# Column-norm attention with a soft mixture of experts on one core: two softmax steps and two small scalings change engine, a fold and a product change form, and the order changes

## The chip, the cores and the metric

The kernel runs on one core of one Trainium2 chip. The core has a matrix engine (TensorE, PE in the profile), a vector engine (VectorE, DVE), an activation engine (ScalarE, ACT), a general engine (GpSimd, POOL), a queue engine that here issues every DMA (SyncE, SP), 24 MB of on-chip memory with 128 partitions (SBUF), and eight accumulator banks (PSUM). The metric is the device time of one execution in microseconds (us); lower is better.

## What is computed

```python
def _attn_ref(q, k, v, tau):            # B, N, C = 4, 5056, 256
    qn = q / (np.linalg.norm(q, axis=1, keepdims=True) + 1e-06)
    kn = k / (np.linalg.norm(k, axis=1, keepdims=True) + 1e-06)
    s = kn.transpose(0, 2, 1) @ qn / tau        # 256 x 256 for each batch
    a = softmax of s over its last axis
    return v @ a                                # x of the next function

def _moe_ref(x, phi, w1, w2):           # x: 20224 rows, 8 experts of 4 slots
    logits = x @ phi                            # 20224 x 32
    d = softmax of logits over the rows
    slot_input = d.T @ x                        # 32 x 256
    h = np.maximum(slot_input[e] @ w1[e], 0.0)  # each expert e, 256 -> 1024
    slot_out[e] = h @ w2[e]                     # 1024 -> 256
    c = softmax of logits over the 32 slots
    return c @ slot_out                         # 20224 x 256
```

All of it is float32. The softmax over the rows needs every row before the experts can begin, and the output needs the experts.

## The kernel before

The rows of q and k come in 40 units of 512 rows, ten for each of the four batches, each as one tile `raw` of 1 MB (two of 0.75 MB). The rows of v come in 20 pairs of 1024 rows, five for each batch (`v`, 1 MB, and for ten of them also a transposed copy `x` read from memory; the other ten are turned by TensorE into tiles `T` and copied to `x` by DVE and ACT). Then come 8 MB of expert weights (`w1`, `w2`) in, and 20.7 MB of output out.

**For each unit** ACT casts `raw` to a rounded high part `hl` (L278), POOL subtracts to get the low part (`low`, L282, 128 partitions x 512 elements a time), ACT squares (L293), DVE adds the squares into two PSUM accumulators `A` (L311), and PE multiplies k by q into the 256 x 256 scores `S` (L335). Some tiles skip the split and go in as plain float32.

**For each batch** the norms are taken, DVE scales the scores (`ssb`, L397) and takes the row maxima (`nm`, L400), ACT takes the exponential (`a`, L406), PE transposes it (`aTp`, L423) and multiplies it with phi (`Mp`, L435), so that the logits of a pair are one product of `x` and `M` (L502), without v @ a ever being formed.

**For each pair** the logits `L` go through ACT and DVE: copies, running maxima, a 32 x 32 stream transpose into `nat` (`logit_nat`, L535; one tile of 128 x 1280 for each batch, 40 groups of 32 slots), exponentials and weights `dn`; PE gathers dn.T @ v (`gather`, L602). At a batch's end the gathered 128 x 256 sum `gs` is folded from four groups of partitions to one (`finish_fold`, L623: two matmuls with a matrix `fold` of four stacked identities), scaled on DVE (`gts`, L629), multiplied with `a` (`sp`, L643) and added to `acc` (L649, L651). For the last batch `acc` is scaled by `be` (L637) and `rz` is formed from the denominators (L668 to L670).

**The softmax over slots**, for each batch on its whole `nat`, has six steps: `c_max` (DVE, L691), `c_sub` (DVE, L694: `nat` minus its maxima broadcast over 32 slots), `c_exp` (ACT, L697), `c_sum` (DVE, L701), `c_rec` (ACT and DVE, L705, L706), `c_mul` (DVE, L709), and then five transposes `c_flip` into `cT` (L721). The maxima `cm` and the sums `cs` have one buffer each for all four batches.

**The tail**: `slT` (L684, L685) holds the transposed slot inputs; `up` is the first expert product (`H`, L746, 64 matmuls), `relu` on ACT (`hs`, L758), `flip_h` and `back_h` (`hTp`, `hT`, L764, L770), `down` in two channel halves (`O0`, `O1`, L779), a copy `ob` (L791), a fold (L795) and `so` (L801), and then the output product of `cT` and `so` (`out_mul`, L817), with evictions by DVE and ACT (L834) and stores (L838 to L843). Batch 0 is stored by channel halves, so that the first half of its output can leave when `O0` is done and before `O1`: tiles `oh` of two pairs and one half, 1 MB (the fifth pair 0.5 MB a half). The other batches are stored as whole pairs `o` of 1 MB.

**What sets the order.** Nothing is scheduled by a rule: the work is a plan of 1201 steps, and a list `ORDER` of their numbers, written out, is the order in which each engine gets its instructions. `SLOTS` gives each large tile one of 23 slots of 8 KB a partition, `BANKS` each PSUM tile one of eight banks. A tile waits for the last users of its slot or bank. All DMAs are issued from SP in `ORDER`'s sequence; each also waits for the DMA eight before it (eight semaphores in turn, DMAHW0 to 7), so a waiting load holds up all behind it. The host lays the inputs out and puts the output's rows back in place.

Of the kernel before, what the change touches and what calls it, by code (L numbers as in the profile page):

```python
# [11 lines left out]
ALU = mybir.AluOpType  # L12
# [155 lines left out]
def colnorm_attention_soft_moe(  # L168
# [450 lines left out]
    def finish_fold(b):  # L619
        gs = st[b]["gs"]  # L620
        gt = bank(f"gt{b}")[:, : 2 * S].rearrange("p (m s) -> p m s", m=2)
        for m in range(2):
            pe.matmul(gt[:, m, :], gs[:, P * m : P * m + P], fold, start=True, stop=True)  # L623
        st[b]["gt"] = gt
# [439 lines left out]
```

## Time and profile before

| | |
|---|---|
| time, median of 3 runs | 280.41 us (280.21 to 280.92) |
| the profiled execution | 280.04 us, of which the span of its trace is 278.1 us |
| busy: PE, DVE, ACT, POOL | 245.0, 219.8, 205.0, 152.6 us |
| DMA | 110.81 MB, mean 398 GB/s over the span |
| read, written | 89.43 MB, 20.97 MB |

The span is the part of the execution that the trace covers; 1.94 us of the profiled execution lie outside it. The engines' busy times overlap, so that they don't add up to the span, and an engine that is busy is not therefore what the end waits for. In the stretches the DMA share is that of sixteen DMA engines that is busy, and the granted clock of TensorE is in shares of full speed (1.00 is 2.4 GHz, 0.50 is 1.2 GHz).

### The profile page before, as it was taken

Reading aid. Unit: us, or ns where it says so; the run is one execution under the profiler, and the core shown is the slowest. Engines: PE = TensorE matmul, PEld = TensorE weight load, DVE = VectorE, ACT = ScalarE, POOL = GpSimd, SP = SyncE. Lnnn points to the kernel's source line nnn. Section 1 sums busy time; section 2 is a strip of 40 time slices with the busy share of each in tenths; the row PEclk is TensorE's granted clock in tenths of the full one; section 3 lists DMA queues with packets and bytes.
Section 4 is the critical chain, followed back from the end, with each engine's and each line's share of the span. In section 5 each row is a group of like instructions: output and inputs, shape, how many; then the busy total and the mean of one; then the engine's idle time right before and its main releaser. Section 6 shows DMA issues by size and latency. Waiting matters only on the chain.

```text
span 278.1 us, 6508 instructions
## 1 busy us (share of the span) xinstructions
PE 245.0 (88%) x2568; PEld 207.8 (75%) x2568; DVE 219.8 (79%) x405; ACT 205.0 (74%) x321; POOL 152.6 (55%) x127
## 2 busy tenths in 40 slices
PE   7999999999999999999992999999999899997000
PEld 6899988999989969798791979996645787765000
DVE  1397498988898998999999999998789969866300
ACT  4999899999999999989963959773727326663200
POOL 1699899999889989999991677600000000000000
PEclk9999999999999999999998699999999999999755
DMA  7999999999999999999999989999999379999996
GB/s 279 430 424 420 420 420 417 421 417 422 420 421 420 422 420 422 413 419 421 417 421 420 415 333 407 428 422 415 416 424 417 132 308 372 411 414 418 424 418 263
DMA packets 15727, 110.81 MB, mean 398 GB/s; under 512 B 1873, under 2 KB 1873, under 8 KB 3025
## 3 DMA queue, kind: packets, MB, share of 16 engines
q1 hardware_dynamic: 15696, 110.40, 96.1%
q8 instruction: 20, 0.33, 0.5%
q14 instruction: 11, 0.08, 0.1%
HBM read 89.43 MB, written 20.97 MB: 397 GB/s over the span
## 4 chain that ended last, share of the span: by engine, by line
PE 40%; DMA 15%; DVE 11%; ACT 11%; POOL 9%; issue 7%; DVEq 0%; ACTq 0%; POOLq 0%
PE S L335 17%; DMA raw<-in_qk_dram 10%; POOL hl L282 9%; PE op_None L817 6%; DVE A L311 5%; DMA w<-in_moe_w_dram 4%; ACT hl L278 4%; PE T L482 4%; ACT sq L293 4%; PE L L502 3%; PE G L602 3%; PE O L779 3%; PE op L817 2%; DVE o L834 2%; ACT o L834 1%
## 5 line engine op out<-in xcount | busy, mean ns | idle before, releaser
L282 POOL TENSOR_TENSOR hl<-raw,hl 128x512 fp32r<-128x512 f32 x117 | 148.2, 1312 | 25.0 <-ACT hl L278 24.4
L311 DVE TENSOR_TENSOR A<-sq,A 128x512 f32<-128x512 f32 (+1 forms) x144 | 94.1, 690 | 20.0 <-ACT sq L293 18.0
L335 PE MATMUL S<-hl 128*128 128x256 f32 x702 | 101.7, 295 | 0.2 <-POOL hl L282 0.2
L335 PEld LDWEIGHTS S<-hl 128*128 128x128 f32 x702 | 90.5, 193 | 3.6 <-issue 2.0
L293 ACT ACTIVATE sq<-raw 128x2048 f32<-128x2048 f32 (+2 forms) x40 | 71.9, 1812 | 0.0
L278 ACT CAST hl<-raw 128x1024 fp32r<-128x1024 f32 (+1 forms) x69 | 61.1, 925 | 2.8 <-DMA raw<-in_qk_dram 1.5
L335 PE MATMUL S<-raw 128*128 128x256 f32 x156 | 38.3, 381 | 0.8 <-DMA raw<-in_qk_dram 0.8
L335 PEld LDWEIGHTS S<-raw 128*128 128x128 f32 x156 | 27.7, 190 | 4.2 <-DMA raw<-in_qk_dram 1.1
L834 DVE COPY o<-op_None 128x512 f32<-128x512 f32 x30 | 18.9, 683 | 7.3 <-PE op_None L817 6.5
L834 ACT COPY o<-op_None 128x512 f32<-128x512 f32 x30 | 15.9, 594 | 10.8 <-PE op_None L817 9.8
L482 PE MATMUL T<-ident,v 128*128 128x128 f32 x156 | 22.9, 281 | 0.0
L602 PE MATMUL G<-v,dn 128*32 128x256 f32 x312 | 19.8, 381 | 0.0
L502 PE MATMUL L<-x,M 128*32 128x256 f32 (+1 forms) x320 | 19.0, 378 | 0.1
L482 PEld LDWEIGHTS T<-ident,v 128*128 128x128 f32 x156 | 18.6, 144 | 0.4
L817 PE MATMUL op_None<-so,cT 32*128 32x256 f32 x160 | 17.8, 405 | 0.4
L817 PEld LDWEIGHTS op_None<-so,cT 32*128 32x128 f32 x160 | 12.1, 183 | 4.8 <-DVE o L834 1.9
L602 PEld LDWEIGHTS G<-v,dn 128*32 128x32 f32 x312 | 11.8, 109 | 4.9
L502 PEld LDWEIGHTS L<-x,M 128*32 128x32 f32 x320 | 9.8, 110 | 6.5 <-issue 0.3
L694 DVE TENSOR_TENSOR nat<-nat,cm 128x1280 f32<-128x1280 f32 x4 | 14.4, 3603 | 0.1
L487 DVE COPY x<-T 128x512 f32<-128x512 f32 x20 | 13.1, 680 | 0.6 <-PE T L482 0.6
L487 ACT COPY x<-T 128x512 f32<-128x512 f32 x20 | 11.3, 588 | 2.3 <-PE T L482 2.3
L817 PE MATMUL op_None<-so,nat 32*128 32x256 f32 x80 | 9.2, 404 | 2.0 <-ACT o L834 0.9
(119 smaller groups left out, 265.2 us busy)
## 6 DMA issues: line engine op xcount, KB each, us to landing
raw<-in_qk_dram SPq DMA_DIRECT2D x38, 1024.0 KB, 13.5
v<-in_v_dram SPq DMA_DIRECT2D x16, 1024.0 KB, 11.6
w<-in_moe_w_dram SPq DMA_DIRECT2D x16, 1024.0 KB, 11.8
out_dram<-o SPq DMA_DIRECT2D x15, 1024.0 KB, 9.6
x<-in_vt_dram SPq DMA_DIRECT2D x10, 1024.0 KB, 13.5
out_dram<-oh SPq DMA_DIRECT2D x4, 1024.0 KB, 5.1
v<-in_v_dram SPq DMA_DIRECT2D x4, 896.0 KB, 15.1
raw<-in_qk_dram SPq DMA_DIRECT2D x2, 768.0 KB, 14.1
```

What stands on the lines that cost most here:

```text
L278: act.copy(parts(u, lo, hi)[:, :, 0::2, :], raws[u][:, lo:hi])
L282: pool.tensor_tensor(hl[:, :, 1::2, :], raws[u][:, lo:hi], hl[:, :, 0::2, :].bitcast(F32), op=ALU.subtract)
L293: act.activation(sqs[u][:, n : NT[u]], raws[u][:, n : NT[u]], AF.Square)
L311: dve.tensor_tensor(a[r], s[r, j], a[r], op=ALU.add)
L335: pe.matmul(S_[:, m], l, r, start=first, stop=False, skip_group_check=True)
L482: pe.transpose(tp[:, P * jj : P * jj + P], vtile(p, 4 * h + jj)[:, P * m : P * m + P], ident)
L487: to(xt(p)[:, m, h * UT : h * UT + UT], tps[p, h, m])
L502: pe.matmul(L[S * g : S * g + S, :n, :], M[:, m, :], x[:, :n, S * g : S * g + S], start=m == 0 and g not in void, stop=m == 1, skip_group_ ...
L602: pe.matmul(gp[S * g : S * g + S, :C], dn[:, x, j, :], vtile(p, j), start=x == 0 and j < G, stop=x == n - 1 and j >= G,)
L694: dve.tensor_tensor(nat[b], nat[b], st[b]["cm"].broadcast_to([P, 8 * PB, S]), op=ALU.subtract)
L817: pe.matmul(ops[b, p, hf, g][:, h, :], cT[b][r, 4 * i : 4 * i + 4, :].rearrange("s j t -> s (j t)"), rhs[r], start=True, stop=True,)
L834: (dve.tensor_copy if g % 2 else act.copy)(dst, ops[b, p, hf, g])
```

## The change

`ORDER`, `SLOTS` and `BANKS` are replaced as a whole. Beside that:

- `c_sub` and `c_mul` go from DVE to POOL, in all four batches.
- The scaling of `acc` by `be` in the last batch and that of `sel_sb` to `rz` go from DVE to ACT.
- `finish_fold` for batches 0 to 2: PE transposes the two halves of `gs` into the bank, and DVE sums the four groups there (a reduction to 128 x 64 from 128 x 256); batch 3 keeps the two matmuls with `fold`.
- `out_mul` for the channel halves: the weights are now the half of `so` (32 x 128) and the moving side is 256 columns of `cT`, so that the result has channels on the partitions; 4 matmuls of 256 columns for a pair and half in place of 8 of 128. Tiles, evictions and stores keep their sizes; the host puts the result in place by another transpose.

```diff
 ORDER = [
-    2, 0, 1, 23, 6, 7, 8, 49, 3, 5, 4, 9, 24, 32, 25, 28, 26, 27, 10, 50, 33, 34, 51, 55, 56, 58, 54, 57, 52,
...
+    2, 3, 0, 1, 6, 8, 4, 7, 9, 5, 23, 32, 24, 25, 26, 33, 29, 49, 28, 30, 50, 51, 56, 54, 55, 10, 11, 12, 18,
...
     def finish_fold(b):
         gs = st[b]["gs"]
-        gt = bank(f"gt{b}")[:, : 2 * S].rearrange("p (m s) -> p m s", m=2)
+        tr = bank(f"gt{b}")
+        st[b]["gt"] = gt = tr[:, C : C + 2 * S].rearrange("p (m s) -> p m s", m=2)
         for m in range(2):
-            pe.matmul(gt[:, m, :], gs[:, P * m : P * m + P], fold, start=True, stop=True)
-        st[b]["gt"] = gt
+            if b < B - 1:
+                pe.transpose(tr[:, P * m : P * m + P], gs[:, P * m : P * m + P], ident)
+            else:
+                pe.matmul(gt[:, m, :], gs[:, P * m : P * m + P], fold, start=True, stop=True)
+        st[b]["tr"] = tr[:, :C].rearrange("p (m g s) -> p m s g", m=2, g=G)
 
     def finish_mul(b):
         gts = bpool.tile([P, 2, S], F32, tag="gts", name=f"gts{b}")
+        if b < B - 1:
+            dve.tensor_reduce(st[b]["gt"], st[b]["tr"], axis=AX.X, op=ALU.add)
         for m in range(2):
...
         if b == B - 1:
-            dve.tensor_scalar_mul(acc, acc, be[:HD])
+            act.mul(acc, acc, be[:HD])
...
-        dve.tensor_scalar_mul(rz, sel_sb, zs)
+        act.mul(rz, sel_sb, zs)
...
     def c_sub(b):
-        dve.tensor_tensor(nat[b], nat[b], st[b]["cm"].broadcast_to([P, 8 * PB, S]), op=ALU.subtract)
+        pool.tensor_tensor(nat[b], nat[b], st[b]["cm"].broadcast_to([P, 8 * PB, S]), op=ALU.subtract)
...
     def c_mul(b):
-        dve.tensor_tensor(nat[b], nat[b], st[b]["cs"].broadcast_to([P, 8 * PB, S]), op=ALU.mult)
+        pool.tensor_tensor(nat[b], nat[b], st[b]["cs"].broadcast_to([P, 8 * PB, S]), op=ALU.mult)
...
     def out_mul(b, p, hf):
-        n = C if hf is None else P
+        so = now["so"]
+        if hf is not None:
+
+            for g in range(G):
+                r = slice(S * g, S * g + S)
+                ops[b, p, hf, g] = bank(f"op{b}_{p}_{hf}_{g}")[:, : 8 * S]
+                pe.matmul(
+                    ops[b, p, hf, g],
+                    so[r, hf],
+                    cT[b][r, 8 * p : 8 * p + 8, :].rearrange("s j t -> s (j t)"),
+                    start=True,
+                    stop=True,
+                )
+            return
         for g in range(G):
-            ops[b, p, hf, g] = bank(f"op{b}_{p}_{hf}_{g}")[:, : 2 * n].rearrange("p (h c) -> p h c", h=2)
-        so = now["so"]
-        rhs = so.rearrange("s x c -> s (x c)") if hf is None else so[:, hf]
+            ops[b, p, hf, g] = bank(f"op{b}_{p}_{hf}_{g}").rearrange("p (h c) -> p h c", h=2)
+        rhs = so.rearrange("s x c -> s (x c)")
```

What the new order moves is shown at three places. In these rows `hl_...`, `raw_...`, `nat_...` are tiles with the program's own numbers, and a line number is that of the kernel whose row it is. `nat_82` and `nat_83` are `nat` of batches 0 and 1; in the kernel after, `nat_2118` and `nat_2432` are those of batches 2 and 3.

**VectorE at the slot softmax of batch 1**, in the kernel before, around the scaling of batch 2's scores (`ssb`, `nm`):

```order
L584 STREAM_TRANSPOSE dn_1_1776<-lt_1_1737 128x512
L311 TENSOR_TENSOR A_0_1475<-sq_1727,A_0_1475 128x512
L649 COPY acc<-sp_1758 64x256
L694 TENSOR_TENSOR nat_83<-nat_83,cm_1671 128x1280
L311 TENSOR_TENSOR A_1_1477<-sq_1699,A_1_1477 128x512
L397 SCALAR_TENSOR_TENSOR ssb_1591<-ssb_1591,rk_1806,rq_1808 128x256
L400 TENSOR_REDUCE nm_1811<-ssb_1591 128x1
```

And VectorE in the kernel after, at the same scaling of batch 2's scores:

```order
L396 SCALAR_TENSOR_TENSOR ssb_1818<-ssb_1818,rk_1869,rq_1862 128x256
L399 TENSOR_REDUCE nm_1871<-ssb_1818 128x1
L654 COPY acc<-sp_1820 64x256
L310 TENSOR_TENSOR A_1_1370<-sq_1910,A_1_1370 128x512
L616 SCALAR_TENSOR_TENSOR gs_1884<-gs_1884,al_1964,G_1_1940 128x256
L696 TENSOR_REDUCE cm_1985<-nat_83 128x40
L310 TENSOR_TENSOR A_0_1368<-sq_1758,A_0_1368 128x512
L310 TENSOR_TENSOR A_1_1370<-sq_1981,A_1_1370 128x512
L310 TENSOR_TENSOR A_0_1368<-sq_1805,A_0_1368 128x512
L416 RECIPROCAL sm_1933<-sm_1933 128x2
```

The subtraction of `nat_83` no longer stands ahead of the scaling, nor on VectorE at all; the maxima of batch 1 (`cm_1985`) now stand behind the scaling, and since `cm` has one buffer they wait for GpSimd's subtraction of batch 0.

**GpSimd from the place where `c_sub` of batch 0 now stands**, in the kernel before the last rows of its program:

```order
L282 TENSOR_TENSOR hl_1960<-raw_1629,hl_1960 128x2x256
L282 TENSOR_TENSOR hl_1962<-raw_1668,hl_1962 128x2x256
L282 TENSOR_TENSOR hl_2071<-raw_1464,hl_2071 128x2x256
L282 TENSOR_TENSOR hl_2077<-raw_1668,hl_2077 128x2x256
L282 TENSOR_TENSOR hl_2071<-raw_1464,hl_2071 128x2x256
L282 TENSOR_TENSOR hl_2174<-raw_1694,hl_2174 128x2x256
L282 TENSOR_TENSOR hl_2177<-raw_1694,hl_2177 128x2x256 x2
L282 TENSOR_TENSOR hl_2174<-raw_1694,hl_2174 128x2x256
L373 TENSOR_TENSOR rn_2200<-rn_2200,half 128x4
```

And GpSimd in the kernel after:

```order
L281 TENSOR_TENSOR hl_1853<-raw_1620,hl_1853 128x2x256
L699 TENSOR_TENSOR nat_82<-nat_82,cm_1366 128x1280
L281 TENSOR_TENSOR hl_1969<-raw_1569,hl_1969 128x2x256
L281 TENSOR_TENSOR hl_1966<-raw_1638,hl_1966 128x2x256 x2
L281 TENSOR_TENSOR hl_2013<-raw_1630,hl_2013 128x2x256
L281 TENSOR_TENSOR hl_1969<-raw_1569,hl_1969 128x2x256
L281 TENSOR_TENSOR hl_2013<-raw_1630,hl_2013 128x2x256
L281 TENSOR_TENSOR hl_2065<-raw_1569,hl_2065 128x2x256 x2
L281 TENSOR_TENSOR hl_1853<-raw_1620,hl_1853 128x2x256
L281 TENSOR_TENSOR hl_2104<-raw_1620,hl_2104 128x2x256
L372 TENSOR_TENSOR rn_2135<-rn_2135,half 128x4
L281 TENSOR_TENSOR hl_2104<-raw_1620,hl_2104 128x2x256
```

The subtraction of batch 0's maxima now stands among the last subtractions of the units, with twelve of them behind it (the twelfth, `hl_2122<-raw_1638`, follows the last row above) and the root of batch 3 (`rn`). Behind that stand the other seven, in this order: `c_sub` of batch 1, `c_mul` of 0, `c_mul` of 1, `c_sub` of 2, `c_sub` of 3, `c_mul` of 2, `c_mul` of 3. On ScalarE the exponential of batch 2's `nat` now stands between `rz` and the four `relu`, and that of batch 3 behind them; both wait for GpSimd.

**SyncE where the last v and the weights are loaded**, with what each load waits for, in the kernel before:

```order
L458 DMA v_2377<-in_v_dram 128x2048 [waits DMAHW1_49,PE_49,Activation_49]
L738 DMA w_0_0_2470<-in_moe_w_dram 128x2048 [waits DMAHW2_49,DVE_49,Activation_49]
L733 DMA w_2_2635<-in_moe_w_dram 128x2048 [waits PE_49,DMAHW3_49,Activation_49,Pool_49]
L733 DMA w_0_2637<-in_moe_w_dram 128x2048 [waits DMAHW4_49,PE_49,Pool_49]
L733 DMA w_4_2657<-in_moe_w_dram 128x2048 [waits DMAHW5_49,PE_49]
```

And in the kernel after:

```order
L457 DMA v_2458<-in_v_dram 128x2048 [waits DMAHW1_49,PE_49]
L743 DMA w_0_3_2587<-in_moe_w_dram 128x2048 [waits DMAHW2_49,Pool_49]
L738 DMA w_3_2638<-in_moe_w_dram 128x2048 [waits DMAHW3_49,PE_49]
L738 DMA w_1_2640<-in_moe_w_dram 128x2048 [waits DMAHW4_49,PE_49]
L738 DMA w_2_2642<-in_moe_w_dram 128x2048 [waits DMAHW5_49,PE_49]
L738 DMA w_4_2670<-in_moe_w_dram 128x2048 [waits DMAHW6_49,PE_49]
```

The load behind the last v now takes the slot that the last subtraction on GpSimd (`hl_2122`) used and waits for it, and six loads of `w1` stand behind it on the queue. In both kernels the last `raw` is the 58th or 59th DMA, the last v the 74th and the last `w1` the 81st, then seven `w2`, then the stores.

## Rows read from the trace of the kernel before

**Rows 1.** The page: busy time of each engine, and what the DMAs moved in each of 40 equal slices of the span.

```profile
PE 245.0 (88%) x2568; PEld 207.8 (75%) x2568; DVE 219.8 (79%) x405; ACT 205.0 (74%) x321; POOL 152.6 (55%) x127
...
GB/s 279 430 424 420 420 420 417 421 417 422 420 421 420 422 420 422 413 419 421 417 421 420 415 333 407 428 422 415 416 424 417 132 308 372 411 414 418 424 418 263
```

**Rows 2.** Stretches of the span: busy time of each engine (and its instructions), granted clock, DMA share, GB/s.

```profile
5.00:140.00 135.00, 134.05 (x1168) 120.50 (x1168) 114.38 (x201) 131.52 (x163) 124.78 (x100) 1.00 1.01 420
140.00:160.00 20.00, 14.34 (x100) 13.61 (x99) 19.83 (x22) 12.88 (x18) 12.11 (x10) 0.83 1.01 418
160.00:170.00 10.00, 10.00 (x133) 8.03 (x133) 9.14 (x18) 7.02 (x13) 6.82 (x7) 1.00 0.93 352
170.00:215.00 45.00, 44.16 (x526) 32.28 (x528) 39.92 (x88) 29.28 (x76) 8.21 (x7) 1.00 1.01 420
215.00:220.00 5.00, 4.23 (x138) 3.77 (x134) 4.38 (x8) 0.34 (x2) 0.00 (x0) 1.00 0.55 226
220.00:225.00 5.00, 5.00 (x146) 4.56 (x142) 4.93 (x12) 2.64 (x9) 0.00 (x0) 1.00 0.51 208
225.00:230.00 5.00, 4.46 (x92) 3.47 (x82) 2.70 (x8) 2.02 (x6) 0.00 (x0) 1.00 0.67 266
230.00:235.00 5.00, 4.67 (x69) 3.76 (x68) 4.79 (x14) 3.03 (x10) 0.00 (x0) 1.00 0.88 361
240.00:275.00 35.00, 15.45 (x156) 10.51 (x154) 14.37 (x24) 11.14 (x21) 0.00 (x0) 0.79 1.01 419
```

**Rows 3.** SP's queue: what its instructions waited for, us in total, times, longest; and its issues in order of time from 136 to 170 and from 205 us (start, length with the waits between, how many).

```profile
SPq L840 <- DVE oh L834: 18.5, 4, 13.1
SPq L458 <- DVE A L311: 18.4, 3, 16.1
...
141.86 20.47 SPq L458 DMA_DIRECT2D v<-in_v_dram  x5
...
172.91 0.33 SPq L458 DMA_DIRECT2D v<-in_v_dram  x1
...
221.71 4.62 SPq L840 DMA_DIRECT2D out_dram<-oh  x2
228.54 0.33 SPq L843 DMA_DIRECT2D out_dram<-oh  x1
230.62 0.33 SPq L838 DMA_DIRECT2D out_dram<-o  x1
```

**Rows 4.** The four `c_sub`: duration in ns, least, median and most, first and last start; then DVE in order of time about the second of them (start, length, what).

```profile
L694 DVE TENSOR_TENSOR nat<-nat,cm x4: 1457/1493/9968, 113.2 to 207.8; 128x1280 f32<-128x1280 f32 x4
...
138.71 9.97 DVE L694 TENSOR_TENSOR nat<-nat,cm 128x1280 f32<-128x1280 f32 x1
148.60 0.68 DVE L311 TENSOR_TENSOR A<-sq,A 128x512 f32<-128x512 f32 x1
```

**Rows 5.** GpSimd in order of time, with the idle time before a group and what ended it; then its five subtractions that began from 110.7 to 117.0 us (duration in ns, least, median, most), among which the first `c_sub` of DVE began at 113.16 and took 1.49 us.

```profile
134.78 12.54 POOL L282 TENSOR_TENSOR hl<-raw,hl 128x512 fp32r<-128x512 f32 x10
154.40 1.28 POOL L282 TENSOR_TENSOR hl<-raw,hl 128x512 fp32r<-128x512 f32 x1 [7.08 <-ACT hl L278]
156.50 8.75 POOL L282 TENSOR_TENSOR hl<-raw,hl 128x512 fp32r<-128x512 f32 x7 [0.81 <-ACT hl L278]
168.42 8.87 POOL L282 TENSOR_TENSOR hl<-raw,hl 128x512 fp32r<-128x512 f32 x7 [3.18 <-ACT hl L278]
177.25 1.01 POOL L373 TENSOR_TENSOR rn<-rn,half 128x4 f32<-128x4 f32 x1
...
L282 POOL TENSOR_TENSOR hl<-raw,hl x5: 1284/1288/2575, 110.7 to 117.0; 128x512 fp32r<-128x512 f32 x5
```

**Rows 6.** ACT and then PE in order of time behind the second `c_sub`, with the idle time and what ended it; and two stretches of 5 us there (columns as in rows 2).

```profile
150.15 0.51 ACT L406 ACTIVATE a<-ssb,nm 128x256 f32<-128x256 f32 x1 [6.88 <-DVE nm L400]
...
150.81 0.44 PE L423 MATMUL aTp<-ident,a 128*128 128x128 f32 x2 [4.05 <-ACT a L406]
153.44 0.69 PE L423 MATMUL aTp<-ident,a 128*128 128x128 f32 x2 [1.60 <-ACT a L406]
...
150.00:155.00 5.00, 2.59 (x14) 2.20 (x15) 4.93 (x10) 4.61 (x9) 0.60 (x1) 0.64 1.01 419
155.00:160.00 5.00, 5.00 (x32) 5.00 (x32) 4.93 (x10) 5.00 (x5) 4.19 (x4) 0.68 0.99 411
```

**Rows 7.** PE in order of time in the tail.

```profile
204.53 7.07 PE L746 MATMUL H<-w,slT 128*32 128x512 f32 x64
214.22 3.70 PE L779 MATMUL O<-w,hT 128*32 128x128 f32 x128
222.34 3.70 PE L779 MATMUL O<-w,hT 128*32 128x128 f32 x128
```

**Rows 8.** The four `c_mul`: duration in ns (least, median, most), first and last start; then two pieces of the chain that ended last (start, length, what, how many).

```profile
L709 DVE TENSOR_TENSOR nat<-nat,cs x4: 1451/1486/1493, 187.7 to 222.0; 128x1280 f32<-128x1280 f32 x4
...
219.18 3.23 PE op L817 x63
245.07 7.65 PE op_None L817 x74
```

**Rows 9.** DVE's scaling of `acc`, which moves to ACT (that of `rz` is shorter), and one of its maxima of a pair's logits, which read 128 x 256 from PSUM.

```profile
L637 DVE TENSOR_SCALAR acc<-acc,be x1: 302/302/302, 200.4 to 200.4; 64x256 f32<-64x256 f32 x1
...
130.74 0.41 DVE L529 TENSOR_REDUCE maxs<-L 128x1 f32<-128x256 f32 x1
```

More of the change, by code (lines that the diff above doesn't have):

```diff
@@ L831, in out_evict @@
             if (p // 2, hf) not in ohs:
-                ohs[p // 2, hf] = slot(f"oh{p // 2}_{hf}", [P, 2, G, 2, P])
+                ohs[p // 2, hf] = slot(f"oh{p // 2}_{hf}", [P, 2, G, 8 * S])
             dst = ohs[p // 2, hf][:, p % 2, g]
@@ L839, in store @@
         elif p < 4:
-            sp.dma_start(oa[p // 2 * 2 + hf], ohs[p // 2, hf].rearrange("p k g h c -> p (k g h c)"))
+            sp.dma_start(oa[p // 2 * 2 + hf], ohs[p // 2, hf].rearrange("p k g t -> p (k g t)"))
         else:
@@ L843, in store @@
             sp.dma_start(
-                oa[4][:, hf * n : hf * n + n], ohs[p // 2, hf][:, 0].rearrange("p g h c -> p (g h c)")
+                oa[4][:, hf * n : hf * n + n], ohs[p // 2, hf][:, 0].rearrange("p g t -> p (g t)")
             )
@@ L1053 @@
     full[1:] = o[PB:].reshape(B - 1, PB, 4, S, G, 2, C)
-    x = o[:4].reshape(2, 2, 4, S, 2, G, 2, P)
-    full[0, :4] = x.transpose(0, 4, 2, 3, 5, 6, 1, 7).reshape(4, 4, S, G, 2, C)
-    x = o[4].reshape(4, S, 2, G, 2, P)
-    full[0, 4] = x.transpose(0, 1, 3, 4, 2, 5).reshape(4, S, G, 2, C)
+    x = o[:4].reshape(2, 2, P, 2, G, 2, 4, S)
+    full[0, :4] = x.transpose(0, 3, 6, 7, 4, 5, 1, 2).reshape(4, 4, S, G, 2, C)
+    x = o[4].reshape(P, 2, G, 2, 4, S)
+    full[0, 4] = x.transpose(4, 5, 2, 3, 1, 0).reshape(4, S, G, 2, C)
     out = full.transpose(0, 1, 5, 2, 4, 3, 6).reshape(B, 8 * PB * P, C)
```

233 rows, old and new, of tables (BANKS, ORDER, SLOTS) are left out of this document.

## The prediction

> **What bounds the kernel now.** I read the page first. PE is busy for 88% of the span, and the DMAs move some 420 GB/s in nearly every slice, with two dents, the deeper at 132 GB/s [rows 1]. A busy engine isn't yet a bound, so I read the stretches next: from 5 to 160 and from 170 to 215 us the DMA share is 1.01 at 418 to 420 GB/s, and again from 240 us to the end [rows 2]. The transfers are the bound, and time is lost only where they stop. Against 420 GB/s, 160 to 170 us lost (420 - 352)/420 x 10 = 1.62 us, and 215 to 235 us lost ((194 + 212 + 154 + 59)/420) x 5 = 7.37 us [rows 2]. With both holes closed the span would be 278.1 - 1.62 - 7.37 = 269.1 us: the floor of any change that leaves the bytes alone.
>
> Then I asked what opened the holes. On SP's queue the longest waits are two: 16.1 us for DVE's adds ahead of a v load, and 13.1 us for DVE's evictions ahead of the first store [rows 3]. The first leads to one instruction: the second `c_sub` took 9.97 us where the median of the four is 1.49 [rows 4]. It began while GpSimd ran ten subtractions without a gap, which ended at 134.78 + 12.54 = 147.32 us, and it ended at 148.6, 1.3 us later [rows 4, 5]. The first `c_sub` shows the other direction: it took 1.49 us and one GpSimd subtraction beside it took 2575 ns in place of 1288 [rows 5]. So a two-input operation of DVE on `nat` and one of GpSimd don't run side by side; the one that comes later stands still. Behind the 9.97 us DVE's adds were late, so raw tiles kept their slots and the loads stopped. ACT sat idle 6.88 us for `nm`, PE 4.05 and 1.60 us for `a`, and then PE ran at a granted clock of 0.64 and 0.68 [rows 6], between its two levels of 1.2 and 2.4 GHz.
>
> The second hole is the tail's. The last load lands when the bytes of 215 to 220 us run out, 226 x 5/420 = 2.69 us in, at 217.7 us [rows 2]; the first store is issued at 221.71 [rows 3]. That store hangs on the chain of experts, which began at t0 = 204.53 (first product `H`) and needs 17.18 us from there to the store [rows 3, 7]. PE was busy 44.16 of the 45 us from 170 to 215 [rows 2], so t0 is late because PE lost time about 150 us.
>
> **The change part by part.** *`c_sub` off DVE.* The 8.5 us go (9.97 - 1.49), and with them three more operations of 1.49; `c_mul` takes four of 1.49 along [rows 4, 8]: some 20 us of DVE. What DVE still does has at most one tensor operand in SBUF, apart from accumulators in PSUM, so I see nothing left to stand still beside GpSimd. PE gets back its idle 5.65 us, and what it lost at the low clock: 2.59 x 0.36 + 5.00 x 0.32 = 2.5 us [rows 6]. By PE alone t0 would be 204.53 - 8.2 = 196.3.
>
> *The eight operations on GpSimd.* None of 128 x 1280 ran there. Nearest is its own subtraction, two inputs of 512 elements in 1288 ns [rows 5]: 1288 x 1280/512 = 3.22 us. Below I bound it by DVE's 1.49 [rows 4], above by the stretched 2575 ns, which gives 6.4 [rows 5]. I take 3.22, since the engine and the operation are the same; the broadcast operand is untried. Only `c_sub` of batch 0 stands among subtractions, with twelve behind it. After 147.32 GpSimd had 15 subtractions and a root of 1.01 us left, and 7.08 + 0.81 + 3.18 us of idle time in which it waited for ACT [rows 5]. Without these it ends at 147.32 + 15 x 1.288 + 1.0 + 3.2 = 170.8 in place of 177.25, 6.4 us earlier. The last scores wait for it, so by GpSimd t0 is 198.1. The later of the two counts: I take t0 = 198.
>
> On paper the move goes the wrong way. The Trainium skill ("GPSIMD Engine Reference", section 3.1, "Elementwise — side-by-side cycle accounting") has GpSimd 1.96 times slower at a two-input operation, 4497 against 2293 ns for 2048 elements, and keeps elementwise work on VectorE. By it one of 1280 is an estimated 2.81 us, t0 is 197.7, and the sum stays; the rule counts an engine's own time, and here the rows price the standstill at 8.5 us.
>
> *The other seven* stand behind the last subtraction, where GpSimd had nothing to do after 178.3 us [rows 2, 5]. `c_sub` of batch 2 is the fourth; ACT's exponential behind it now stands ahead of the four relu. It ends at 170.8 + 4 x 3.2 = 183.7 or whenever its logits allow, both ahead of the relu, which can't run before the banks of `H` fill, from about t0 + 5 on (`H` takes 7.07 us for its four banks) [rows 7]. Seven operations at 6.4 us would cover 45 us, and then the margin is gone (below).
>
> *New waits.* `cm` has one buffer, so DVE's `c_max` of batch 1 waits for GpSimd's `c_sub` of batch 0. Queued behind it are adds, two turned copies and the reciprocal of batch 2's sums, for which ACT and then PE wait. The wait can be nothing (GpSimd is ahead) up to one subtraction and the operation itself, 1.3 + 3.2 = 4.5 us; I take nothing beyond the 198.1, because the same GpSimd operation is counted there. On SP the load behind the last v waits for GpSimd's last subtraction, with six w1 loads behind it. A gap of 16.1 us in the issues lost 1.6 us of transfer [rows 2, 3], so the cover is some 14.5 us: the last v, issued at 172.91 - 1.6 = 171.3 us, covers until 185.8, and the last subtraction ends near 171. No cost.
>
> *Small parts.* Halves of the output: 80 matmuls of 256 columns at 7.65/74 = 103 ns are 8.2 us, 160 of 128 at 3.23/63 = 51 ns are 8.2 [rows 8]; nothing. Fold: three reductions of 128 x 256 from PSUM at 0.41 us [rows 9] on a DVE that has given up 20; nothing. `acc` and `rz` on ACT: 0.30 us at most [rows 9]; hidden, since ACT waits there for PE.
>
> *The sum.* With no stall the first hole closes, 1.62 us. Loads then end at 217.7 - 1.6 = 216.1. The first store comes at 198 + 17.2 = 215.2, ahead of that, so the second hole's front closes; it would reopen one for one from t0 = 198.9. Two stores of 1 MB carry the transfers to 221.1. `O1` needs the last load, so it ends at about 216.1 + 1.9 = 218.0 (half of its 3.70 us); the next stores came 2.50 and 4.58 us behind its end [rows 3, 7], at 220.5 and 222.6. The 0.5 MB of the first lasts until 222.3. What stays is about 0.3 us there, and up to 1 us if the second store follows the first by its old 4.3 us; I keep 1.3 us. Span: 269.1 + 1.3 = 270.4. The profiled execution had 280.04 - 278.1 = 1.94 us outside its span, and the median of the runs is 0.37 above it: 270.4 + 1.94 + 0.37 = **272.7 us**.
>
> **The rivals.** *A partial gain.* DVE waits for GpSimd at `c_max`, or GpSimd's operation takes up to 6.4 us: t0 comes at 199 to 204, and each us beyond 198.9 is lost in the tail: 274 to 278 us, at t0 = 202 about 276. For it speaks that GpSimd had no gap from 134.78 to 147.32 [rows 5] and now gets more to do there; against it the 11 us of idle time right behind.
>
> *No change.* The 9.97 us have another cause than GpSimd, or the new order brings another standstill of that size: 280.4. The Trainium skill ("SBUF — State Buffer", section "SBUF: two separate sides") tells of one port pair that VectorE with two SBUF inputs and GpSimd lock for a whole instruction, the first one keeping it. By that rule the standstill can't come back, as VectorE keeps no such instruction; the trace agrees with it in both directions [rows 4, 5], which is why this rival gets little.
>
> *Slower: GpSimd becomes the bound.* If the broadcast operand makes one operation p us, the last subtraction ends at 167.6 + p and `c_sub` of batch 2 at 167.6 + 5p. ACT's exponential waits for that and the four relu stand behind it. Before, `H` ended at 211.6 [rows 7] and the relu with it; an exponential that waits for `c_sub` until about then gives the old tail back. 167.6 + 5p is 211.6 at p = 8.8 us: from there it is slower, by 5 us for each us of p, and at 10 us the time is 280.4 + 5 x 1.2 = 286. Against it: that is 2.7 times what the subtraction's rate gives.
>
> **How the numbers follow.** Forecast (271 to 274): 0.54. Partial gain (274 to 278.5): 0.24. No change: 0.08. Slower: 0.14. The first two are faster by over 0.3%, which is about what this measurement can tell from no change: 0.78; within 0.3%: 0.08; slower 0.14. The range reaches from the floor (269.1 + 2.3 = 271.4, less the scatter of the transfers' rate) to the end of no change: 270.5 to 280.5, which leaves out the slower case and little else.
>
> **What would show it.** Right: no DVE operation over 2 us; PE without an idle stretch near 150 and its granted clock at 1.00 there; DMA at 420 GB/s through 160 to 170; the first store ahead of the last load's landing, and under 2 us of transfer lost between 210 and 235; GpSimd's operations at 3 to 3.5 us. Wrong: DVE idle before `c_max` with GpSimd named; relu waiting for the exponential of batch 2 and that for GpSimd; `H` starting after 200; or a new dent in the GB/s elsewhere.

## The result and the profile after

The kernel after takes **273.65 us** (median of 4 runs, 273.60 to 273.69) beside 280.67 for the kernel before: a ratio of 0.9751 (95% interval 0.9733 to 0.9768). The forecast was 272.7. The profiled execution took 273.62 us, 271.8 of them span. Of 46 executions of the kernel before that ran beside all the kernels told of here, 34 took 279.4 to 282.0 us and 12 took 273.5 to 275.2; the ratio and the comparisons below are with the former, beside the latter the change gains nothing, and ten executions of the kernel after all took 273.5 to 273.8.

The page of the kernel after, the lines that answer to [rows 1]:

```profile
PE 241.1 (89%) x2482; PEld 203.6 (75%) x2482; DVE 200.5 (74%) x398; ACT 205.4 (76%) x323; POOL 169.9 (62%) x135
...
GB/s 270 429 426 418 421 423 417 424 404 422 424 418 423 420 422 418 420 416 417 421 417 426 419 421 417 418 421 418 420 422 420 386 317 410 416 418 412 418 423 231
```

VectorE gave up 19.3 us and GpSimd took on 17.3. Of the two dents one is gone and the other is 317 GB/s deep in place of 132. The stretches that answer to [rows 2] (busy us of each engine, granted clock, DMA share, GB/s):

```profile
140.00:160.00 20.00, 20.00 (x208) 17.35 (x210) 19.33 (x38) 18.98 (x32) 19.44 (x16) 1.00 1.02 422
160.00:170.00 10.00, 9.91 (x117) 8.61 (x106) 8.10 (x20) 5.92 (x12) 9.57 (x8) 1.00 1.01 419
...
210.00:215.00 5.00, 4.22 (x91) 3.34 (x84) 2.36 (x8) 1.64 (x7) 0.00 (x0) 1.00 0.96 397
215.00:220.00 5.00, 4.86 (x138) 3.99 (x133) 4.30 (x13) 1.13 (x5) 2.35 (x1) 1.00 0.87 362
220.00:225.00 5.00, 4.53 (x56) 3.96 (x59) 3.84 (x10) 3.19 (x9) 0.00 (x0) 1.00 0.75 305
225.00:230.00 5.00, 5.00 (x65) 4.45 (x58) 4.69 (x11) 3.86 (x10) 0.00 (x0) 1.00 1.02 413
```

PE is busy for all 20 us from 140 to 160, where it was busy for 14.34, at a granted clock of 1.00 in place of 0.83. Against 420 GB/s, 210 to 230 us loses (23 + 58 + 115 + 7)/420 x 5 = 2.4 us, where 215 to 235 lost 7.37.

GpSimd in order of time, and DVE at the place of the new wait (start, length, what, idle time before):

```profile
141.97 7.53 POOL L281 TENSOR_TENSOR hl<-raw,hl 128x512 fp32r<-128x512 f32 x6
149.46 2.34 POOL L699 TENSOR_TENSOR nat<-nat,cm 128x1280 f32<-128x1280 f32 x1
151.76 3.77 POOL L281 TENSOR_TENSOR hl<-raw,hl 128x512 fp32r<-128x512 f32 x3
156.09 8.75 POOL L281 TENSOR_TENSOR hl<-raw,hl 128x512 fp32r<-128x512 f32 x7 [0.56 <-ACT hl L277]
165.27 1.01 POOL L372 TENSOR_TENSOR rn<-rn,half 128x4 f32<-128x4 f32 x1 [0.43 <-DVE rn L367]
166.25 2.55 POOL L281 TENSOR_TENSOR hl<-raw,hl 128x512 fp32r<-128x512 f32 x2
...
152.66 0.48 DVE L616 SCALAR_TENSOR_TENSOR gs<-gs,al,G 128x256 f32<-128x256 f32 x1
153.06 1.48 DVE L696 TENSOR_REDUCE cm<-nat 128x40 f32<-128x1280 f32 x1
```

`c_sub` of batch 0 takes 2.34 us and is over at 151.8. `c_max` of batch 1, which waits for it, starts at 153.06 right behind DVE's operation before it: the wait cost nothing. The last subtraction ends at 168.8 in place of 177.3.

The tail, answering to [rows 3, 7] (PE, then SP's first stores, then two pieces of the chain that ended last):

```profile
197.27 8.77 PE L751 MATMUL H<-w,slT 128*32 128x512 f32 x64
207.94 3.70 PE L784 MATMUL O<-w,hT 128*32 128x128 f32 x128
...
215.15 3.80 SPq L857 DMA_DIRECT2D out_dram<-oh  x2
222.54 0.33 SPq L860 DMA_DIRECT2D out_dram<-oh  x1
...
202.67 15.33 DMA w<-in_moe_w_dram
218.04 1.97 PE O L784 x60
```

`H` starts at 197.27, 7.3 us earlier, and the first store leaves at 215.15, 6.6 us earlier and ahead of the last load. That load lands at 218.0, and `O1` can't finish before 220.0.

### The profile page after: what moved, and what is told of

Its sections match the earlier page's. It is cut to its first block, busy times and chain, and to the rows that moved or that the text cites. A ratio compares the mean times of both kernels' runs of the same rounds, so it can differ in the third digit from the quotient of the medians.

```text
span 271.8 us, 6334 instructions
## 1 busy us (share of the span) xinstructions
PE 241.1 (89%) x2482; PEld 203.6 (75%) x2482; DVE 200.5 (74%) x398; ACT 205.4 (76%) x323; POOL 169.9 (62%) x135
## 4 chain that ended last, share of the span: by engine, by line
PE 77%; DMA 7%; DVE 4%; ACT 2%; issue 1%; DVEq 0%
PE S L334 45%; PE T L481 7%; PE L L501 6%; DMA w<-in_moe_w_dram 6%; PE op_None L834 5%; PE G L601 4%; DVE o L851 2%; PE H L751 2%; DMA raw<-in_qk_dram 2%; PE op L819 2%; PE Mp L434 1%; ACT o L851 1%; PE S L343 1%; PE O L784 1%; PE nn L362 1%
## 5 line engine op out<-in xcount | busy, mean ns | idle before, releaser
L310 DVE TENSOR_TENSOR A<-sq,A 128x512 f32<-128x512 f32 (+1 forms) x144 | 93.7, 690 | 21.2 <-ACT sq L292 19.3
L334 PE MATMUL S<-hl 128*128 128x256 f32 x702 | 98.4, 292 | 0.0
L334 PEld LDWEIGHTS S<-hl 128*128 128x128 f32 x702 | 88.8, 191 | 2.6 <-issue 1.2
L334 PE MATMUL S<-raw 128*128 128x256 f32 x156 | 39.9, 396 | 0.8 <-DMA raw<-in_qk_dram 0.8
L334 PEld LDWEIGHTS S<-raw 128*128 128x128 f32 x156 | 29.3, 199 | 5.2 <-DMA raw<-in_qk_dram 1.1
L714 POOL TENSOR_TENSOR nat<-nat,cs 128x1280 f32<-128x1280 f32 x4 | 9.4, 2346 | 29.9 <-DVE cs L711 20.9
L851 DVE COPY o<-op_None 128x512 f32<-128x512 f32 x30 | 19.3, 682 | 4.8 <-PE op_None L834 4.7
L481 PE MATMUL T<-ident,v 128*128 128x128 f32 x156 | 21.4, 274 | 0.0
L601 PE MATMUL G<-v,dn 128*32 128x256 f32 x312 | 19.3, 381 | 0.0
L834 PE MATMUL op_None<-so,cT 32*128 32x256 f32 x160 | 15.5, 402 | 0.6 <-ACT o L851 0.5
L834 PEld LDWEIGHTS op_None<-so,cT 32*128 32x128 f32 x160 | 10.9, 184 | 3.3 <-ACT o L851 2.0
L699 POOL TENSOR_TENSOR nat<-nat,cm 128x1280 f32<-128x1280 f32 x4 | 9.4, 2344 | 2.9 <-DVE zs L673 2.9
```

The costliest lines, as they stand in the source:

```text
L310: dve.tensor_tensor(a[r], s[r, j], a[r], op=ALU.add)
L334: pe.matmul(S_[:, m], l, r, start=first, stop=False, skip_group_check=True)
L481: pe.transpose(tp[:, P * jj : P * jj + P], vtile(p, 4 * h + jj)[:, P * m : P * m + P], ident)
L601: pe.matmul(gp[S * g : S * g + S, :C], dn[:, x, j, :], vtile(p, j), start=x == 0 and j < G, stop=x == n - 1 and j >= G,)
L699: pool.tensor_tensor(nat[b], nat[b], st[b]["cm"].broadcast_to([P, 8 * PB, S]), op=ALU.subtract)
L834: pe.matmul(ops[b, p, hf, g][:, h, :], cT[b][r, 4 * i : 4 * i + 4, :].rearrange("s j t -> s (j t)"), rhs[r], start=True, stop=True,)
```

## The experiments

All were run beside the kernel before; medians of 4 executions, with the least and the most, unless said otherwise.

### Only `c_sub` on GpSimd, in the old order

```diff
     def c_sub(b):
-        dve.tensor_tensor(nat[b], nat[b], st[b]["cm"].broadcast_to([P, 8 * PB, S]), op=ALU.subtract)
+        pool.tensor_tensor(nat[b], nat[b], st[b]["cm"].broadcast_to([P, 8 * PB, S]), op=ALU.subtract)
```

> The kernel before with one edit: the four c_sub on GpSimd, old order, tables and everything else. Theory standstill (the 9.97 us op of VectorE waited for GpSimd's subtractions; whatever takes it off VectorE brings the gain): no VectorE operation over 2 us on nat, TensorE without the idle 5.6 us about 150, granted clock 1.00 there, first expert product H at 196 to 199 in place of 204.5, time 273 to 276.5. Theory order (the gain comes from the new order and its tables): the time stays at 279.5 to 281.

Measured: 276.29 us (275.47 to 277.06). The theory of a standstill is right and the order's is wrong: without any of the new tables, one edit takes 4 us off. Two of the expected signs didn't come. `H` starts at 199.50 us, half a microsecond later than expected (and takes 8.77 us, at a granted clock of 0.69 from 200 to 205 us), and one VectorE operation on `nat` still takes over 2 us, a `c_mul` beside GpSimd's last `c_sub`:

```profile
203.00 2.35 POOL L694 TENSOR_TENSOR nat<-nat,cm 128x1280 f32<-128x1280 f32 x1 [27.42 <-DVE cm L691]
203.13 3.56 DVE L709 TENSOR_TENSOR nat<-nat,cs 128x1280 f32<-128x1280 f32 x1
```

So moving `c_sub` alone also brings a new standstill in.

### `c_sub` of batch 1 later, on VectorE

```diff
 ORDER = [
-    ... 985 (c_sub 1) ... 995 (c_max 2) ... 986 (c_exp 1) ... 941 (att_pow 3) ...
+    ... 941 (att_pow 3), 985 (c_sub 1), 986 (c_exp 1), 995 (c_max 2) ...
```

> The kernel before with c_sub and c_exp of batch 1, and c_max of batch 2 behind them, moved in the order to behind the root of batch 3, which is GpSimd's last work; all stay on their engines, VectorE does as much as before. Theory standstill: c_sub of batch 1 takes 1.49 us at about 172 to 178, no stall about 140 to 150, time 273 to 276.5. Rival (VectorE had to be relieved of work, so the engine of c_sub matters): time over 278.

Measured: 276.16 us (275.36 to 278.19). Here VectorE does all that it did before, and the time is that of the run with GpSimd. So what counted in the middle was not VectorE's load but the meeting with GpSimd's subtractions. Why this run and the one before it stay some 2.5 us above the kernel after wasn't separated; here `H` starts at 199.96.

### The new order with `c_sub` on VectorE

```diff
     def c_sub(b):
-        pool.tensor_tensor(nat[b], nat[b], st[b]["cm"].broadcast_to([P, 8 * PB, S]), op=ALU.subtract)
+        dve.tensor_tensor(nat[b], nat[b], st[b]["cm"].broadcast_to([P, 8 * PB, S]), op=ALU.subtract)
```

> The kernel after with the four c_sub back on VectorE, in the same order and places. Theory standstill: only c_sub of batch 0, at about 152, meets GpSimd's subtractions; either it stands still there (3 to 6 us) or it starts between two of them and one of GpSimd's takes about 2.6 us; the other three take 1.49; the time is 273.6 to 276. Theory relief (each c_sub off VectorE pays): 275 to 278, with VectorE late in the tail too.

Measured: 275.38 us (275.31 to 276.94), within what either theory allowed. The operation's four durations (least, median, most):

```profile
L699 DVE TENSOR_TENSOR nat<-nat,cm x4: 1427/1466/1758, 152.0 to 207.3; 128x1280 f32<-128x1280 f32 x4
```

VectorE's operation hardly stood still, but GpSimd's did: one subtraction took 2.52 us beside the first `c_sub`, as [rows 5] had it before. The kernel is 1.7 us slower than the kernel after, and `H` starts at 200.10 instead of 197.27. On the way PE waits four times for VectorE (0.22, 0.27, 0.68 and 0.97 us from 154 to 178 us), and in the kernel after not once there. So relief of VectorE seems worth something in the new order; its share wasn't separated from that of GpSimd's lost 1.2 us.

### One input in SBUF

The constant stands in for the row maxima, so batch 1's maxima are left out of that subtraction.

```diff
     def c_sub(b):
+        if b == 1:
+            dve.tensor_scalar_add(nat[b], nat[b], -0.125)
+            return
```

> The kernel before, but c_sub of batch 1 subtracts a constant in place of the row maxima: one tensor input on VectorE, same place in the order, same 128 x 1280 elements. It leaves out batch 1's maxima in that subtraction. Theory that it takes two inputs in SBUF for the standstill: the operation takes at most 1.5 us, the time is 273 to 276.5. Rival (any VectorE operation from SBUF to SBUF stands still beside GpSimd's subtractions): about 10 us again and 279.5 to 281.

Measured: three of four executions at 280.25 to 281.92 us, one at 273.43. VectorE and GpSimd in order of time:

```profile
139.79 9.60 DVE L695 TENSOR_SCALAR nat<-nat 128x1280 f32<-128x1280 f32 x1
149.31 0.68 DVE L311 TENSOR_TENSOR A<-sq,A 128x512 f32<-128x512 f32 x1
...
136.19 12.52 POOL L282 TENSOR_TENSOR hl<-raw,hl 128x512 fp32r<-128x512 f32 x10
```

My theory that it takes two inputs in SBUF fell: an operation with one tensor input stood still for 9.60 us all the same, until 149.39, 0.68 us after GpSimd's run of ten ended at 148.71. `c_sub` in the kernel before ended 1.3 us behind GpSimd [rows 4, 5], so by these ends it also does its elements about twice as fast once it runs. Yet not every VectorE operation on SBUF is held: `c_max` and the transposes ran beside GpSimd's subtractions at their usual length in every trace here.

### The maxima in PSUM

```diff
     def c_max(b):
-        st[b]["cm"] = bpool.tile([P, 8 * PB, 1], F32, tag="cm", name=f"cm{b}")
+        st[b]["cm"] = now["cm1"] if b == 1 else bpool.tile([P, 8 * PB, 1], F32, tag="cm", name=f"cm{b}")
...
     def logits(p):
-        L = bank(f"L{p}")[:, : 8 * S].rearrange("p (j s) -> p j s", s=S)
+        Lb = bank(f"L{p}")
+        if p == 9:
+            now["cm1"] = Lb[:, 8 * S : 8 * S + 8 * PB].rearrange("p (j x) -> p j x", x=1)
+        L = Lb[:, : 8 * S].rearrange("p (j s) -> p j s", s=S)
```

> The kernel before with one edit: batch 1's maxima are written by VectorE into unused columns of a PSUM bank (that of its last logits) in place of SBUF, so that c_sub of batch 1 stays on VectorE at its old place among GpSimd's subtractions, but has one input in SBUF and one in PSUM. After the run with one SBUF input (9.60 us, in the faster mode of VectorE, 0.68 us behind GpSimd's end) the theory is: what stands still beside GpSimd is an operation of VectorE with two inputs in SBUF or one that runs in VectorE's fast mode. Theory: this c_sub takes 1.4 to 1.8 us, no stall about 140 to 150, time 273 to 277. Rival (any long VectorE operation that reads and writes nat in SBUF stands still): about 10 us again, time 279.5 to 281.5.

Measured: **273.62 us** (273.46 to 274.08), the time of the kernel after. VectorE's `c_sub` of batch 1 and GpSimd's subtractions around it:

```profile
138.97 1.46 DVE L697 TENSOR_TENSOR nat<-nat,L 128x1280 f32<-128x1280 f32 x1
...
135.38 13.79 POOL L282 TENSOR_TENSOR hl<-raw,hl 128x512 fp32r<-128x512 f32 x11
```

At the old place in the old order, beside eleven subtractions without a gap, the operation takes 1.46 us in place of 9.97, and none of the subtractions takes over 1.30 us, so neither side waited. Nothing is moved to GpSimd and nothing is reordered; where its second operand lies decides. That settles the cause.

### The new order with `c_mul` on VectorE

```diff
     def c_mul(b):
-        pool.tensor_tensor(nat[b], nat[b], st[b]["cs"].broadcast_to([P, 8 * PB, S]), op=ALU.mult)
+        dve.tensor_tensor(nat[b], nat[b], st[b]["cs"].broadcast_to([P, 8 * PB, S]), op=ALU.mult)
```

> The kernel after with the four c_mul back on VectorE, same order; they run behind GpSimd's last subtraction. The prediction's working: they lie beside other work, so 273.4 to 274.2, no change. Rival (VectorE is what the tail waits for): c_mul of batches 2 and 3 stand ahead of hT and of the evictions, the first store leaves 1 to 2 us later, 274.5 to 276.

Measured: 275.89 us (275.36 to 277.08): the rival. The place isn't the tail, as that rival had it, but ahead of `H` (DVE, then PE with its idle time):

```profile
185.87 1.45 DVE L714 TENSOR_TENSOR nat<-nat,cs 128x1280 f32<-128x1280 f32 x1
...
193.08 1.49 DVE L714 TENSOR_TENSOR nat<-nat,cs 128x1280 f32<-128x1280 f32 x1
...
190.07 1.07 PE L601 MATMUL G<-v,dn 128*32 128x256 f32 x16 [1.08 <-DVE top L550]
194.98 1.71 PE L601 MATMUL G<-v,dn 128*32 128x256 f32 x27 [1.08 <-DVE dn L583]
```

Batch 0's `c_mul` now stands ahead of the last maxima and batch 1's ahead of the last weights, and for each PE waits 1.08 us; `H` starts at 199.69.

### The new order with the small parts undone

```diff
-            if b < B - 1:
-                pe.transpose(tr[:, P * m : P * m + P], gs[:, P * m : P * m + P], ident)
...
-            act.mul(acc, acc, be[:HD])
+            dve.tensor_scalar_mul(acc, acc, be[:HD])
...
-        act.mul(rz, sel_sb, zs)
+        dve.tensor_scalar_mul(rz, sel_sb, zs)
```

> The kernel after with three parts undone: the fold of batches 0 to 2 by two matmuls again, the scaling of acc and that of rz on VectorE again. By the prediction these are worth nothing: 273.3 to 274.1. Rival: ACT's 0.52 us for acc is on the chain of waits ahead of H (0.29 us of idle TensorE), so up to 0.5 us faster, and if TensorE's granted clock then stays at 1.00 through H (8.77 us there, 7.07 before), up to 1 us faster.

Measured: 276.75 us (276.37 to 277.05), 3.1 slower; neither theory had it. DVE, GpSimd and PE:

```profile
194.19 2.24 DVE L636 TENSOR_SCALAR acc<-acc,be 64x256 f32<-64x256 f32 x1 [0.40 <-ACT be L633]
...
201.73 2.21 DVE L669 TENSOR_SCALAR rz<-few_sb,zs 128x2 f32<-128x2 f32 x1
...
193.94 2.34 POOL L693 TENSOR_TENSOR nat<-nat,cm 128x1280 f32<-128x1280 f32 x1
201.58 2.34 POOL L693 TENSOR_TENSOR nat<-nat,cm 128x1280 f32<-128x1280 f32 x1 [5.29 <-DVE zs L667]
...
196.58 0.63 PE L658 MATMUL slp<-fold,acc 64*128 64x32 f32 x4 [1.97 <-DVE acc L636]
...
200.04 9.69 PE L745 MATMUL H<-w,slT 128*32 128x512 f32 x64
```

The scaling of `acc`, 0.302 us in the kernel before [rows 9], takes 2.24: it begins 0.25 us behind a GpSimd operation and ends with it, and PE waits 1.97 us. `rz`, two elements wide, takes 2.21 us beside another. It is the same standstill, brought in by GpSimd's new work. It isn't all of the 3.1 us: PE waits 0.29 us for `acc` in the kernel after too, so this wait is 1.7 us longer, and `H` takes 9.69 us for 8.77, at a granted clock of 0.50 from 200 to 205 us, the lower of the two levels, where the kernel after had 0.93. `rz` cost nothing that shows: the last `relu` waits for `H` in both. What the fold alone is worth wasn't separated.

### The new order with the halves multiplied as before

```diff
     def out_mul(b, p, hf):
-                pe.matmul(ops[b, p, hf, g], so[r, hf], cT[b][r, 8 * p : 8 * p + 8, :] ...)
+                pe.matmul(ops[b, p, hf, g][:, h, :], cT[b][r, 4 * i : 4 * i + 4, :] ..., rhs[r] ...)
```

> The kernel after with batch 0's halves multiplied as before: 160 matmuls of 128 columns with the slots' output on columns, in place of 80 of 256 with channels on partitions; order, tiles and stores as after. By the prediction nothing: 273.3 to 274.2. Rival: the first half's products are in the chain ahead of the first two stores (2.94 us for 32 after, 3.23 us for 64 before), so 0.3 us slower per store, 274 to 274.5.

Measured: 274.15 us (273.77 to 274.51). That is 0.5 us above the kernel after and less than this measurement can tell from no change; its sign stays open.

### Three tries at the rest of the hole

The kernel after once more, and two that move batch 0's fifth pair and some evictions ahead:

> The kernel after, unchanged, beside the next two on the same chip: 273.5 to 273.8 us.

```diff
 ORDER = [
-    ... down 0 1 0 to 6, down 1 1 0 to 6, o_copy 1, o_fold 1, out_mul 0 4 0, ..., store 0 4 0 ...
+    ... down 0 1 0 to 6, out_mul 0 4 0, its evictions, store 0 3 0, store 0 4 0, down 1 1 0 to 6 ...
```

> The kernel after with the product, evictions and store of batch 0's fifth pair, first half, moved from behind O1 to the middle of O1 (before the part that waits for the last load). Theory (what is left of the tail's hole is the third store, which three kernels of 273.6 to 274.2 us all issue at 222.5 us because O1 waits for the last load at 218.0): the third store leaves at 219 to 220, the empty stretch at 222 to 223.4 us shrinks by about 1 us, time 272.4 to 273.0. Rival (the extra matmuls and evictions push the stores behind O1 later by as much): 273.5 to 274.

The next one also takes three transposes of batches 1 and 2 (`c_flip`) out from between the second store's evictions:

> The same, and VectorE's evictions for the second store stand ahead of three transposes in place of behind them. Theory: the second store leaves about 1 us earlier (217.6 in place of 218.6), which fills the dip of 218 to 220 us (0.3 us of transfer): 272.0 to 272.8. Rival (the transposes are needed sooner): as the run before it, or up to 0.5 us slower.

Measured (6 executions each): 273.59 (273.47 to 273.78), 273.59 (273.45 to 273.93) and 274.37 (273.49 to 276.08). The third store left at 219.28, as expected, and nothing was won. SP, and two stretches, of the second of the three:

```profile
219.28 0.33 SPq L859 DMA_DIRECT2D out_dram<-oh  x1
224.13 0.33 SPq L854 DMA_DIRECT2D out_dram<-o  x1
...
222.00:223.00 1.00, 1.00 (x23) 0.66 (x16) 0.22 (x1) 0.32 (x1) 0.00 (x0) 1.00 0.99 401
224.00:225.00 1.00, 1.00 (x17) 0.94 (x17) 1.00 (x5) 0.77 (x4) 0.00 (x0) 1.00 0.20 82
```

The hole went from 222 to 224: the fourth store leaves at 224.13, in the kernel after at 223.91, since it needs `O1`. Until then there are the loads and 2.5 MB to move, in whatever order. In the third of the runs the second store did leave earlier, at 217.37 for 218.62, and that won nothing either. The last run tried to end `O1` sooner:

```diff
     def down(r, h, f0):
-        for f in (f0, f0 + 1):
-            for g in range(G):
+        late = [(f, f0 // 4 * 2 + g) for f in range(f0 % 4 * 2, f0 % 4 * 2 + 4) for g in range(2)]
+        for f, g in late if (r, h) == (1, 1) else [(f, g) for f in (f0, f0 + 1) for g in range(G)]:
```

> The kernel after with one edit: in the second half of O1 the 16 products that need the last but one load come first and the 16 that need the last load after them, in place of alternating. In the kernel after all but two of the 32 wait for the last load, which lands at 218.0 us, and take 1.94 us from there. Theory (O1's end sets what is left of the hole, since the run with the third store moved only shifted the hole behind it): O1 ends about 1 us sooner, at 219.0, every store from the third on leaves about 1 us sooner, time 272.4 to 272.9. Rival (the hole is set by the bytes that are ready, or the products of one pair of groups take twice as long each): 273.4 to 273.8.

Measured: 274.30 us (273.53 to 276.23, 13 executions); no gain. In its profiled execution, which was also its longest, `O1` takes longer (answering to 3.70 us in [rows 7]):

```profile
217.63 5.04 PE L784 MATMUL O<-w,hT 128*32 128x128 f32 x128
```

By the time it started its loads had all but landed, so it shows no more than that products which alternate between two groups of partitions don't run as fast as with four. None of these kernels beats the kernel after, or the kernel before with its maxima in PSUM.

## Why the prediction was right, and where it was off

**The cause in the middle: right, and too narrow.** That `c_sub` of batch 1 stood still for GpSimd and that its removal would give PE and the loads back is shown by three kernels of their own: 276.29 with it on GpSimd, 276.16 with it later, 273.62 with one operand in PSUM. The forecast had t0 = 198 and it is 197.27; the first hole closed as the sum had it (419 to 422 GB/s). But I wrote that it takes two tensor operands in SBUF, "so I see nothing left to stand still beside GpSimd". The run with one input and the 2.2 us of `acc` and `rz` refute that. The page that the prediction cited (the Trainium skill, "SBUF — State Buffer", here its section "Who interferes with whom") is wider than what I took from it: it names VectorE's operations in a two-port mode too, with `tensor_scalar` among those that can enter one, and says that one SBUF input outside those modes doesn't contend. The traces agree, though none shows the mode: `tensor_scalar` 9.60 us, one operand in PSUM 1.46 us, the reduction 1.48.

**GpSimd's operation: mis-sized without effect.** 2.34 us, not 3.22 scaled from its subtractions, so the sign of 3 to 3.5 us didn't come; the estimate of 2.81 by the Trainium skill ("GPSIMD Engine Reference", section 3.1) was nearer. GpSimd's last subtraction ended at 168.8, 2.0 us ahead of the sum's 170.8, 0.9 of them by this. `c_sub` of batch 2 ended at 196.3 and not at 183.7, since two `c_mul` ahead of it waited 8.96 and 9.23 us for VectorE; that cost nothing either, as the last `relu` still waits for `H`. The new waits cost nothing, as forecast, and on SP the load behind the last v was issued right as the last subtraction ended, without a loss of transfer.

**"Small parts: nothing": wrong.** The step costed `acc` and `rz` at 0.30 us from the trace of before, where GpSimd was idle in the tail. The change itself puts GpSimd there, and then they stand still for 2.2 us each, of which PE pays 1.7 us for `acc`. The step that failed is to price an operation by its old neighbour. Likewise `c_mul` was lumped into 20 us of relief without a place; undone, it costs 2.2 us through two waits of PE of 1.08. So the moves to ACT and GpSimd hold the gain in the new order, rather than add to one: where nothing stands still, as with the maxima in PSUM, the kernel before has the same 273.6 us without any of them.

**The tail: right in its front, 1.1 us short behind.** The first store was forecast for 215.2 and left at 215.15, by luck in part: `H` began 0.7 us before the forecast's 198, and from there to the store it took 17.9 us and not 17.2, since `H` took 8.77 us for 7.07. The hole that stays was forecast at 1.3 us and measures 2.4, so the sign "under 2 us of transfer lost" didn't come. The term that was mis-sized is the last load's landing: 216.1 in the sum, 218.0 measured. The step behind it read the row of 215 to 220 us as if the loads ran at 420 GB/s to their last byte, and so had the last load of the kernel before land at 217.7. It lands at 219.4 there, because the transfers run out at a falling rate. Three stretches and the last load of the kernel before (its issue, then the time to its landing):

```profile
216.00:217.00 1.00, 1.00 (x48) 1.00 (x43) 1.00 (x2) 0.00 (x0) 0.00 (x0) 1.00 0.96 401
217.00:218.00 1.00, 0.92 (x36) 0.65 (x24) 0.41 (x3) 0.00 (x0) 0.00 (x0) 1.00 0.53 213
218.00:219.00 1.00, 0.49 (x2) 0.30 (x2) 1.00 (x4) 0.14 (x1) 0.00 (x0) 1.00 0.20 82
...
L738 SPq DMA_DIRECT2D w<-in_moe_w_dram x1: 328/328/328, 208.2 to 208.2; - x1
DMA to landing us min/median/max: 11.2/11.2/11.2
```

The change brought the landing forward by 1.4 us, near the 1.6 of the sum; the time that this was taken off was wrong. It isn't the early first store that holds the last load up. With the halves multiplied as before the first store leaves at 213.71, with the small parts undone at 218.84, and the last load lands at 218.0 to 218.1 in both (first store, last load's issue and time to landing of the one, then of the other):

```profile
213.71 3.80 SPq L845 DMA_DIRECT2D out_dram<-oh  x2
L743 SPq DMA_DIRECT2D w<-in_moe_w_dram x1: 328/328/328, 201.0 to 201.0; - x1
DMA to landing us min/median/max: 17.0/17.0/17.0
...
218.84 3.80 SPq L851 DMA_DIRECT2D out_dram<-oh  x2
L737 SPq DMA_DIRECT2D w<-in_moe_w_dram x1: 328/328/328, 206.4 to 206.4; - x1
DMA to landing us min/median/max: 11.7/11.7/11.7
```

In every trace here whose first hole is closed it lands from 218.0 to 218.3. With the landing, `O1`'s end (220.0 for 218.0) and the stores behind it moved, and the last three tries show that the hole shifts but doesn't close while `O1` waits.

**The rest of the difference.** 272.7 + 1.1 is 273.8; the other terms cancel to 0.15: the span is 0.3 us longer than that, 0.1 less lies outside it, and the median of the runs is 0.03 above the profiled execution, not 0.37.

## What to carry to other kernels

An operation that takes seven times its usual length in one place can be a meeting of two engines and not a load: look at what the other engine runs at that moment, and change the operand (PSUM in place of SBUF), the place or the engine, whichever is cheapest; here two edited places in the source did what a new order did. When work is moved to GpSimd, every VectorE operation that will lie beside it has a new price, the small ones on the critical path first. And where transfers are the bound, an earlier store helps only until something behind it waits for the last load: here a first store 1.4 us earlier still (213.71 for 215.15) won nothing. When that load lands is read from its own landing, not from bytes over the full rate.

## What was not expected of the hardware

- Small operations stand still too: 128 x 2 elements took 2.21 us beside a GpSimd operation of 2.34 where alone it took 0.23. And a standstill lasts through a whole run of GpSimd's operations: the 9.97 us reach over some seven subtractions of 1.29.
- The standstill seems not to come in every execution of the same program: the shorter times of the kernel before, and the 273.43 us with one input, are those of kernels without one. No trace of such an execution was taken, so this is argued from the times.
- TensorE's granted clock fell as `H` began in the kernel after (0.73 from 195 to 200 us, between the levels of 1.2 and 2.4 GHz; 0.72 in its second trace), and stayed at 1.00 in the kernel that differs from it only in the form of the halves' products, far behind. Stretches from 195 to 200 us, after, then that kernel:

```profile
195.00:200.00 5.00, 4.66 (x31) 2.56 (x34) 3.18 (x9) 0.84 (x3) 2.10 (x2) 0.73 1.01 423
```

```profile
195.00:200.00 5.00, 4.66 (x43) 2.70 (x46) 3.17 (x9) 0.85 (x3) 2.10 (x2) 1.00 1.01 421
```

  TensorE was busy 4.66 of 5 us in both, and 4.71 of the 5 before that. `H` took 8.77 us in one and 7.09 in the other. Why isn't known; the time doesn't show it, since `O1` waits for the last load either way.
- The on-chip memory is larger than the 24 MB named at the start: the 23 slots of 8 KB in each of the 128 partitions are 23 MB by themselves, and with the tiles beside them (`nat`, constants, small ones) either kernel lays out some 27 MB.
